# The radix-2 step of a second DFT stage moved onto the tokens, its constant factor stationary in eight 64x32 tiles of TensorE

## The chip, the cores and the metric

The kernel runs on one core of one Trainium2 chip. The metric is the device time of one execution in microseconds (us); lower is better. The median of three runs is compared, and one execution of each kernel is also recorded by the hardware profiler.

## The reference

```python
# x [8, 2496, 256], filt_r and filt_i [1249, 256]: all float32
X = np.fft.rfft(x, axis=1)
Y = X * (filt_r + 1j * filt_i)[None]
y = np.fft.irfft(Y, n=2496, axis=1)
x = y.reshape(8 * 2496, 256)
# soft mixture of experts: 8 experts, 4 slots each, 32 slots; phi [256, 32]
logits = x @ phi
d = softmax of logits over the 19968 tokens, one per slot
slot_out = relu((d.T @ x) @ w1) @ w2      # per expert: w1 [256, 1024], w2 [1024, 256]
c = softmax of logits over the 32 slots, one per token
out = c @ slot_out
```

## The kernel before

A DFT over 2496 = 39 x 64 tokens is computed as two stages. The first is a DFT over 39 for each of 64 residues; only 20 of its 39 frequencies t are needed, because x is real. The second is a DFT over 64 for each of the 20 t. The filter is applied to the spectra, and the logits and the slot inputs are taken from the spectra, so the inverse DFT is done only on the 32 slots' logits, not on the 256 channels.

The work of a batch entry b (8 of them, in order) is cut into these units:

- `split_x` (L299 to L307): ScalarE casts a tile of x to fp32r (`xh`, L305) and GpSimd takes the remainder `xl` (L306), 117 partitions by 512 elements each, 11 times for each b from 1 on.
- `s1_unit` (L309 to L324): the first DFT stage. Three fp32r matmuls of 512 columns (L316) accumulate `w1h*xh + w1l*xh + w1h*xl`; ScalarE copies the result to `at` (L317), and a DMA writes it to DRAM (`a_dram`, L321 to L324).
- `load_ash` (L331 to L338): a DMA reads two t back from `a_dram` with (residue, real or imaginary part) on the partitions.
- `x_unit` (L340 to L364): the second DFT stage for two t. The data tile `ash` is the stationary operand (128x128) and the constant 128x128 matrix `b` moves (128 columns), so the spectra stand in PSUM with channels on the partitions. VectorE multiplies them by the filter's real part (L360) and imaginary part (L361), VectorE or GpSimd (b from 6 on) adds (L363), and GpSimd subtracts (L364).
- `t_unit` (L366 to L390): four TensorE transposes turn the two t (L372), ScalarE copies them to `y` (L374), with frequencies on the partitions; at every second unit eight matmuls in 32-column tiles form logit spectra from phi (L383), and ScalarE copies them (L390).
- `chain(g)` (L396 to L607): for groups of b (0 and 1, 2 and 3, 4 and 5, 6, 7), the inverse DFT of the logits, the maximum, the exponentials, the forward DFT of the dispatch weights (`u2` L529, `dd` L537), and the slot sums (L575). It is a generator, advanced a few steps ("hops") per slot.

For b = 0 the first stage is done without DRAM by `first_unit` (L273 to L280) and `turn_ash` (L282 to L293).

One loop (L703 to L730) runs 80 slots, ten per b: slot n issues `load_ash` for slot n+5 (`ASH`), `split_x` for the next slot, `x_unit` of slot n, `s1_unit` for a later b (`AHEAD` 5 slots before), `t_unit` of slot n-2 (`LT`), and two or three hops. Instructions go to each engine's queue in an order that the framework plans from its own estimates; program order is not kept strictly. All DMAs are issued by SP's one queue. PSUM has eight banks, two for each of four pools (`ps_s1`, `ps_x`, `ps_t`, `ps_c`); a result of `x_unit` takes one bank, so two can be in flight.

After the loop come the last chains, the loads of w1 and w2 into freed buffers (L731 to L743), the experts (L762 to L800) and the output stage: softmax weights are turned and multiplied by the slot outputs (L859), copied (L868) and written (L891).

```python
# x_unit, before
pe.matmul(ps[:, 2 * k + dh].rearrange("q r c -> q (r c)"),
          ash[:, k, dh * P : (dh + 1) * P], C("b"), start=True, stop=True)
```

Of the kernel before, what the change touches and what calls it, by code (L numbers as in the profile page):

```python
# [9 lines left out]
F32 = mybir.dt.float32  # L10
# [33 lines left out]
KP = N2 + 2  # L44

XC = 4
XB = 3
AB = 5
AHEAD = 5
ASH = 5  # L50
LT = 2
HOPS = 2
LATE_HOPS = 3
# [3 lines left out]
X0S = 4  # L57
PA = 6
YB = 34
# [18 lines left out]
def bin_of(t, c):  # L78

    m = (c - t * pow(N1, -1, N2)) % N2  # L80
    return t + N1 * m


def shape_constants():
# [10 lines left out]
    th = 2 * np.pi * (np.outer(s2, N1 * np.arange(N2)) % N2) / N2  # L95
    co, si = np.cos(th), np.sin(th)
    bm = np.zeros((N2, 2, 2, N2))
    bm[:, 0, 0], bm[:, 0, 1], bm[:, 1, 0], bm[:, 1, 1] = co, -si, si, co
    bm = np.where(np.abs(bm) < 1e-12, 0.0, bm).reshape(P, P)
    wh = np.ones((P, 1))  # L100
    wh[0] = wh[N2 // 2] = 0.5
    minv = np.zeros((P, KP * 2))
    minv[:, 0:P] = SCALE * bm.T
    minv[:, P:] = np.tile(minv[:, P - 2 : P], (1, KP - N2))

# [15 lines left out]
    put("b", bm)  # L121
    put("wh", wh)
    put("minv", minv)
    put("minv0", wh * minv)
# [33 lines left out]
def filter_layout(filt):  # L158

    f = np.array([[bin_of(t, c) for c in range(N2)] for t in range(NT)])  # L160
    a = filt[np.where(f > SEQ // 2, SEQ - f, f)]
    a[0, N2 // 2 + 1 :] = 0
    return np.ascontiguousarray(a.reshape(NT, N2, 2, P).transpose(3, 0, 2, 1)).reshape(P, NT * 2 * N2)


def flip_runs(t):

    out = []
    for c in range(N2):
        if bin_of(t, c) > SEQ // 2:  # L170
            if out and out[-1][1] == c:
                out[-1] = (out[-1][0], c + 1)
            else:
                out.append((c, c + 1))
    return out


def x_layout(x):

    s1 = np.arange(N1)  # L180
    full = np.zeros((BATCH, P, NI, DIM), x.dtype)
# [22 lines left out]
def fft_soft_moe(ctx, tc, x, fr, fi, phi, w1, w2, cst, w1q, out):  # L204
# [12 lines left out]
    w1h = const.tile([KR, QP], F32R, name="w1h")  # L217
    w1l = const.tile([KR, QP], F32R, name="w1l")
    nc.vector.tensor_copy(w1h, w1q_t)
    nc.vector.tensor_tensor(out=w1l, in0=w1q_t, in1=w1h.bitcast(F32), op=ALU.subtract)  # L220

# [28 lines left out]
    fr_t = tabs.tile([P, NT, 2, 64], F32, name="fr_t")  # L250
    fi_t = tabs.tile([P, NT, 2, 64], F32, name="fi_t")
# [3 lines left out]
    def load_x(b, c):  # L255
        if b == 0:
            t = ypool.tile([P, 2, DIM], F32, tag="y", name=f"xt0_{c}")
            sp.dma_start(t, x[0, :, 2 * c : 2 * c + 2, :])
        else:
            t = proda.tile([P, XC, DIM], F32, tag="xt", name=f"xt{b}_{c}", bufs=XB)  # L260
            i0 = c * XC
            n = min(XC, NI - i0)
            sp.dma_start(t[:, 0:n, :], x[b, :, i0 : i0 + n, :])
        xts[b, c] = t

    def first_unit(u):

        xt = xts.pop((0, u))
        pool, tag = ((ps_s1, "s1"), (ps_x, "x"))[u % 2]
        ps = pool.tile([P, 2, 2, QP], F32, tag=tag, name=f"s0_{u}")  # L270
        for i in range(2):
            for dh in range(2):
                pe.matmul(ps[:, dh, i, :], xt[0:KR, i, dh * P : (dh + 1) * P], w1q_t, start=True, stop=True)  # L273
        n = min(2 * PK, N2 - 2 * PK * u)
        to = spec[:, :, :, 4 * PK * u : 4 * PK * u + 2 * n].rearrange("d h t k -> d h k t")
        src = ps.rearrange("d h i (j r t) -> d h (i j r) t", r=2, t=NT)[:, :, 0 : 2 * n]
        if u % 2 == 1:
            dve.tensor_copy(to, src)
        else:
            act.copy(to, src)  # L280

    def turn_ash(c):  # L282

        pt = ps_c.tile([P, 2, DIM], F32, tag="c", name=f"ash0_{c}")
        for k in range(2):
            for dh in range(2):
                pe.transpose(pt[:, k, dh * P : (dh + 1) * P], spec[:, dh, 2 * c + k, :], ident)
        ash = prod.tile([P, 2, DIM], F32, tag="ash", name=f"ash0_{c}", bufs=ASH)
        if c % 2 == 0:
            dve.tensor_copy(ash, pt)  # L290
        else:
            act.copy(ash, pt)
        ashs[0, c] = ash  # L293
# [3 lines left out]
    xhl = {}  # L297

    def split_x(b, u):  # L299

        c, k = divmod(2 * u, XC)
        xs = xts[b, c][0:KR, k : k + 2, :]
        xh = proda.tile([KR, 2, DIM], F32R, tag="xh", name=f"xh{b}_{u}", bufs=3)
        xl = proda.tile([KR, 2, DIM], F32R, tag="xl", name=f"xl{b}_{u}", bufs=3)
        act.copy(xh, xs)  # L305
        pool_e.tensor_tensor(out=xl, in0=xs, in1=xh.bitcast(F32), op=ALU.subtract)  # L306
        xhl[b, u] = xh, xl  # L307

    def s1_unit(b, u):  # L309
        if u == 0:  # L310
            a_dram[b] = scr.tile([N2, QR, DIM], F32, tag="a_dram", name=f"a_dram{b}")
        xh, xl = xhl.pop((b, u))
        ps = ps_s1.tile([QP, 2, DIM], F32, tag="s1", name=f"s1_{b}_{u}")
        at = proda.tile([QP, 2, DIM], F32, tag="at", name=f"at{b}_{u}", bufs=AB)
        for n, (w, xx) in enumerate(((w1h, xh), (w1l, xh), (w1h, xl))):
            pe.matmul(ps, w, xx, start=(n == 0), stop=(n == 2))  # L316
        act.copy(at, ps)  # L317
        k0 = PK * 2 * u
        dma = sp.dma_start
        if u < NH - 1:  # L320
            dma(a_dram[b][k0 : k0 + 2 * PK].rearrange("(i j) q d -> (j q) i d", j=PK), at)  # L321
        else:
            dma(a_dram[b][k0 : k0 + PK].rearrange("j q d -> (j q) d"), at[:, 0, :])
            dma(a_dram[b][k0 + PK], at[0:QR, 1, :])  # L324
# [6 lines left out]
    def load_ash(b, c):  # L331
        if b == 0:
            turn_ash(c)
            return
        t0 = 2 * c
        ash = prod.tile([P, 2, DIM], F32, tag="ash", name=f"ash{b}_{c}", bufs=ASH)
        sp.dma_start(ash, a_dram[b].rearrange("k (r t) d -> (k r) t d", t=NT)[:, t0 : t0 + 2, :])
        ashs[b, c] = ash  # L338

    def x_unit(b, c):  # L340

        t0 = 2 * c
        ash = ashs.pop((b, c))
        ps = ps_x.tile([P, 4, 2, 64], F32, tag="x", name=f"x_{b}_{c}")
        for k in range(2):
            for dh in range(2):
                pe.matmul(  # L347
                    ps[:, 2 * k + dh].rearrange("q r c -> q (r c)"),
                    ash[:, k, dh * P : (dh + 1) * P],
                    C("b"),  # L350
                    start=True,
                    stop=True,
                )
# [3 lines left out]
        if c % 2 == 0:  # L357
            yts[b, c // 2] = prod.tile([P, 2, 4, 2, 64], F32, tag="yt", name=f"yt_{b}_{c}")
# [565 lines left out]
```

## Time and profile before

| | before |
|---|---|
| runs (us) | 395.42, 400.12, 400.64; median 400.12 |
| profiled execution (us) | 398.73 |
| span in its profile (us) | 397.0 |
| mean granted TensorE clock | 0.95 |
| TensorE busy | 367.3 us, 93% of the span |
| VectorE, ScalarE, GpSimd busy | 67%, 54%, 52% of the span |
| moved by DMA | 103.67 MB, 261 GB/s over the span |

The span runs from the first to the last instruction; the execution's own time is 1.7 us longer. In the profile PE is TensorE's matmuls, PEld its weight loads (which overlap matmuls), DVE VectorE, ACT ScalarE, POOL GpSimd, SP the engine that issues DMAs. L347 is line 347 of the kernel. A float32 matmul stands in the profile as two records, each with a weight load of its own; a transpose or an fp32r matmul stands as one. A group's row gives busy time and the mean duration of one record; records of one group overlap, so that busy time is less than count times duration.

### The profile page before, as it was taken

Reading aid. Unit: us, or ns where it says so; the run is one execution under the profiler, and the core shown is the slowest. Engines: PE = TensorE matmul, PEld = TensorE weight load, DVE = VectorE, ACT = ScalarE, POOL = GpSimd, SP = SyncE. Lnnn points to the kernel's source line nnn. Section 1 sums busy time; section 2 is a strip of 40 time slices with the busy share of each in tenths; the row PEclk is TensorE's granted clock in tenths of the full one; section 3 lists DMA queues with packets and bytes.
Section 4 is the critical chain, followed back from the end, with each engine's and each line's share of the span. In section 5 each row is a group of like instructions: output and inputs, shape, how many; then the busy total and the mean of one; then the engine's idle time right before and its main releaser. Section 6 shows DMA issues by size and latency. Waiting matters only on the chain. (4 is left out here: it accounts for less than half of the span.)

```text
span 397.0 us, 11950 instructions
## 1 busy us (share of the span) xinstructions
PE 367.3 (93%) x4797; PEld 292.8 (74%) x4797; DVE 267.8 (67%) x465; ACT 215.3 (54%) x454; POOL 206.7 (52%) x258
## 2 busy tenths in 40 slices
PE   7998989998998999999989999999998899989980
PEld 6886778887686868887868688886766435889870
DVE  2496589874999928698996458994577222874570
ACT  2665858784667566757675343462455020654460
POOL 0499989994676666846945155662520000622200
PEclk9999999999999999999999999999999699985595
DMA  7997799997688886977886534423399993599796
GB/s 249 363 288 252 245 328 384 373 372 264 173 230 316 269 252 188 338 205 247 280 271 200 178 108 123 120 81 107 108 364 352 322 304 125 236 414 409 322 407 282
DMA packets 57481, 103.67 MB, mean 261 GB/s; under 512 B 5375, under 2 KB 34175, under 8 KB 55251
## 3 DMA queue, kind: packets, MB, share of 16 engines
q1 hardware_dynamic: 57427, 102.92, 77.1%
q8 instruction: 38, 0.62, 0.6%
q14 instruction: 16, 0.13, 0.1%
HBM read 62.78 MB, written 40.12 MB: 259 GB/s over the span
## 5 line engine op out<-in xcount | busy, mean ns | idle before, releaser
L306 POOL TENSOR_TENSOR xl<-xt,xh 117x512 fp32r<-117x512 f32 x77 | 102.0, 1332 | 17.8 <-ACT xh L305 17.3
L347 PE MATMUL x<-cst_t,ash 128*128 128x128 f32 x640 | 89.9, 281 | 3.2 <-issue 1.7
L347 PEld LDWEIGHTS x<-cst_t,ash 128*128 128x128 f32 x640 | 80.2, 191 | 12.8 <-issue 6.6
L364 POOL TENSOR_TENSOR yt<-yt,t 128x256 f32<-128x256 f32 x80 | 64.8, 812 | 39.4 <-DVE t L361 21.2
L360 DVE TENSOR_TENSOR yt<-x,fr_t 128x512 f32<-128x512 f32 x80 | 54.7, 683 | 29.7 <-PE x L347 16.4
L305 ACT CAST xh<-xt 117x512 fp32r<-117x512 f32 x77 | 47.6, 623 | 30.5 <-PE s L316 13.5
L374 ACT COPY y<-t 128x512 f32<-128x512 f32 x80 | 46.0, 590 | 29.1 <-PE t L372 27.4
L361 DVE TENSOR_TENSOR t<-x,fi_t 128x512 f32<-128x512 f32 x80 | 54.4, 680 | 2.4 <-POOL yt L364 2.2
L363 DVE TENSOR_TENSOR yt<-yt,t 128x256 f32<-128x256 f32 x60 | 51.0, 860 | 0.5
L372 PE MATMUL t<-cst_t,yt 128*128 128x128 f32 x320 | 48.5, 276 | 0.0
L317 ACT COPY at<-s 120x512 f32<-120x512 f32 x77 | 45.2, 587 | 4.6 <-PE s L316 4.1
L372 PEld LDWEIGHTS t<-cst_t,yt 128*128 128x128 f32 x320 | 37.3, 141 | 7.3 <-issue 2.7
L859 PE MATMUL out<-so_h,st 32*128 32x256 f32 x312 | 36.2, 355 | 3.1 <-ACT st L813 2.7
L316 PE MATMUL s<-xh,w1h 117*120 117x512 f32 x77 | 35.6, 462 | 2.1 <-ACT at L317 1.4
L859 PE MATMUL out<-so_l,st 32*128 32x256 f32 x312 | 34.3, 331 | 0.0
L825 POOL TENSOR_TENSOR c<-cl,r_all 117x352 f32<-117x352 f32 x8 | 6.2, 798 | 53.5 <-PE ct L839 46.8
L859 PEld LDWEIGHTS out<-so_h,st 32*128 32x128 f32 x312 | 29.8, 234 | 5.5 <-ACT st L813 3.1
L868 DVE COPY ob<-out 128x512 f32<-128x512 f32 (+1 forms) x40 | 25.4, 673 | 11.5 <-PE out L859 11.0
L316 PE MATMUL s<-xl,w1h 117*120 117x512 f32 x77 | 31.3, 407 | 0.0
L868 ACT COPY ob<-out 128x512 f32<-128x512 f32 (+1 forms) x40 | 21.5, 579 | 16.9 <-PE out L859 14.6
L316 PE MATMUL s<-xh,w1l 117*120 117x512 f32 x77 | 30.6, 397 | 0.0
L363 POOL TENSOR_TENSOR yt<-yt,t 128x256 f32<-128x256 f32 x20 | 16.2, 810 | 27.3 <-DVE t L361 15.0
(110 smaller groups left out, 566.3 us busy)
## 6 DMA issues: line engine op xcount, KB each, us to landing
xt<-in_x SPq DMA_DIRECT2D x35, 512.0 KB
ash<-a_dram SPq DMA_DIRECT2D x70, 256.0 KB
out<-ob SPq DMA_DIRECT2D x17, 1024.0 KB
a_dram<-at SPq DMA_DIRECT2D x70, 240.0 KB
w<-in_w SPq DMA_DIRECT2D x64, 256.0 KB
xt<-in_x SPq DMA_DIRECT2D x18, 256.0 KB
out<-ob SPq DMA_DIRECT2D x5, 512.0 KB
c_dram<-lg SPq DMA_DIRECT2D x2, 643.5 KB
```

The lines of the kernel that those rows point to most:

```text
L305: act.copy(xh, xs)
L306: pool_e.tensor_tensor(out=xl, in0=xs, in1=xh.bitcast(F32), op=ALU.subtract)
L316: pe.matmul(ps, w, xx, start=(n == 0), stop=(n == 2))
L347: pe.matmul(ps[:, 2 * k + dh].rearrange("q r c -> q (r c)"), ash[:, k, dh * P : (dh + 1) * P], C("b"), start=True, stop=True,)
L360: dve.tensor_tensor(out=yt, in0=ps, in1=frv, op=ALU.mult)
L361: dve.tensor_tensor(out=t2, in0=ps[:, :, ::-1, :], in1=fiv, op=ALU.mult)
L363: add.tensor_tensor(out=yt[:, :, 1, :], in0=yt[:, :, 1, :], in1=t2[:, :, 1, :], op=ALU.add)
L364: pool_e.tensor_tensor(out=yt[:, :, 0, :], in0=yt[:, :, 0, :], in1=t2[:, :, 0, :], op=ALU.subtract)
L372: pe.transpose(pt[:, k, dh, :], yt[:, c % 2, 2 * k + dh].rearrange("q r c -> q (r c)"), ident)
L374: act.copy(y, pt.rearrange("k p h d -> k p (h d)"))
L859: nc.tensor.matmul(prs[k][:, mm, :], st[q, n // 2, c0 : c0 + P], (so_h, so_l)[n % 2][q, :], start=(n == 0), stop=(n == 3),)
L868: copy(ob[:, nm * k : nm * (k + 1), :], prs[k])
```

## The change

The 64 residues k are taken as two halves, k and k + 32. The first butterfly of the DFT over 64 is done on the tokens, before the first stage: e = x(k) + x(k+32) and x(k) - x(k+32). The sums give the even frequencies of the second stage and the differences the odd ones, and each needs a sum over 32 residues x 2 parts = 64 rows only. In detail:

- `split_x` is replaced by `fold_x`: two tensor_tensor of 117 x 2 x 256 elements on GpSimd (for b = 0 the sum is on VectorE), the difference written in place. There is no cast to fp32r any more, and `s1_unit` uses one float32 matmul per result instead of three fp32r ones.
- `x_unit` handles four t: the constant `bx` is now the stationary operand in tiles of 64 rows x 32 columns (two halves of the rows x four column groups), the data `ash` moves with 256 columns. The spectra come out with frequencies on the partitions. The result takes two banks, and `ps_x` has one buffer of two banks instead of two of one.
- `y` is written by the filter's multiplications directly; `t_unit` turns it to channels on the partitions for the logits, with the same number of transposes and copies. Logits are taken for groups of two and three units, so with fewer, longer bursts and copies.
- The filter tables have the new layout; the signs of `fi_t` are set by ten ScalarE multiplications instead of GpSimd ones on column runs.
- In `chain`, `dd` is formed by 32-column tiles of `bd` stationary, and the half weight of two bins is applied to `lsb` by VectorE rather than by a second constant.
- There are 40 slots of twice the size; `AHEAD`, `ASH`, `LT`, hops and buffer counts are set anew.

```diff
-AHEAD = 5
-ASH = 5
-LT = 2
-HOPS = 2
-LATE_HOPS = 3
+EB = 2
+AHEAD = 3
+ASH = 2
+YT = 4
+LT = 1
+HOPS = 4
+LATE_HOPS = 6
...
-    ps_x = ctx.enter_context(tc.tile_pool(name="ps_x", bufs=2, space=PSUM))
+    ps_x_cm = tc.tile_pool(name="ps_x", bufs=1, space=PSUM)
+    ps_x = ps_x_cm.__enter__()
...
-        act.copy(xh, xs)
-        pool_e.tensor_tensor(out=xl, in0=xs, in1=xh.bitcast(F32), op=ALU.subtract)
+        e = proda.tile([P, 2, DIM], F32, tag="e", name=f"e{b}_{c}", bufs=EB)
+        eng = dve if b == 0 else pool_e
+        eng.tensor_tensor(out=e[0:KR, 0:n], in0=xt[0:KR, 0:n, 0], in1=xt[0:KR, 0:n, 1], op=ALU.add)
+        pool_e.tensor_tensor(out=xt[0:KR, 0:n, 1], in0=xt[0:KR, 0:n, 0], in1=xt[0:KR, 0:n, 1], op=ALU.subtract)
...
-        for n, (w, xx) in enumerate(((w1h, xh), (w1l, xh), (w1h, xl))):
-            pe.matmul(ps, w, xx, start=(n == 0), stop=(n == 2))
-        act.copy(at, ps)
+        for h, xe in enumerate(folds.pop((b, c))):
+            pe.matmul(ps[:, 0:n], w1q_t, xe[0:KR, 0:n], start=True, stop=True)
+            act.copy(at[:, 0:n], ps[:, 0:n])
...
-        ps = ps_x.tile([P, 4, 2, 64], F32, tag="x", name=f"x_{b}_{c}")
-        for k in range(2):
-            for dh in range(2):
-                pe.matmul(
-                    ps[:, 2 * k + dh].rearrange("q r c -> q (r c)"),
-                    ash[:, k, dh * P : (dh + 1) * P],
-                    C("b"),
+        ps = ps_x.tile([P, 2, 2, DIM], F32, tag="x", name=f"x_{b}_{c}")
+        for r in range(2):
+            for j in range(4):
+                for h in range(2):
+                    rows = slice(N2 * h, N2 * h + N2)
+                    pe.matmul(
+                        ps[NP * j : NP * j + NP, h, r],
+                        C("bx", NP * r, NP * r + NP)[rows],
+                        ash[rows, j],
...
-        dve.tensor_tensor(out=yt, in0=ps, in1=frv, op=ALU.mult)
+        dve.tensor_tensor(out=y, in0=ps, in1=frv, op=ALU.mult)
         dve.tensor_tensor(out=t2, in0=ps[:, :, ::-1, :], in1=fiv, op=ALU.mult)
...
+        for dh in range(2):
+            pt = ps_t.tile([P, 4, P], F32, tag="t", name=f"t_{b}_{c}_{dh}")
+            for k in range(4):
+                pe.transpose(pt[:, k, :], y[:, k // 2, k % 2, dh * P : (dh + 1) * P], ident)
+            act.copy(yt[:, dh], pt)
...
+            first = lsb[:, b2, 0]
+            dve.tensor_scalar(out=first, in0=first, scalar1=C("wh"), scalar2=None, op0=ALU.mult)
...
+        for c0 in range(0, 4, step):
+            pd = psum([P, step, NG4, nb * SLOTS], f"dd_{g}_{c0}")
+            for k in range(step):
+                for j in range(4):
+                    pe.matmul(
+                        pd[32 * j : 32 * j + 32, k],
+                        C("bd", 32 * (c0 + k), 32 * (c0 + k) + 32),
+                        u2[:, j::4],
...
-                pool_e.tensor_scalar(out=sl, in0=sl, scalar1=-1.0, scalar2=None, op0=ALU.mult)
+            act.mul(fi_t[:, c, h], fi_t[:, c, h], C("sg", 2 * c + h, 2 * c + h + 1))
```

More of the change, by code (lines that the diff above doesn't have):

```diff
@@ L56 @@
 WM = 1
-X0S = 4
+X0S = 1
 PA = 6
-YB = 34
+YB = 17
 WL = 5
@@ L93, in shape_constants, with turn @@
             w1[:, 1, t] = -np.sin(th)
[L95 to L99, printed above, removed]
+    def turn(k, f2):
+        th = 2 * np.pi * (np.outer(k, f2) % N2) / N2
+        co, si = np.cos(th), np.sin(th)
+        m = np.stack([np.stack([co, -si], 1), np.stack([si, co], 1)], 1)
+        return np.where(np.abs(m) < 1e-12, 0.0, m)
+    odd = 2 * np.arange(NP)
+    bx = np.stack([turn(np.arange(NP), odd + e) for e in range(2)]).reshape(P, 2 * NP)
+    bd = np.stack([turn(s2, odd + e) for e in range(2)], 2).reshape(P, P)
     wh = np.ones((P, 1))
-    wh[0] = wh[N2 // 2] = 0.5
+    wh[0] = wh[NP // 2] = 0.5
     minv = np.zeros((P, KP * 2))
-    minv[:, 0:P] = SCALE * bm.T
+    minv[:, 0:P] = SCALE * bd.T
     minv[:, P:] = np.tile(minv[:, P - 2 : P], (1, KP - N2))
+    sg = np.ones((4, NP, NG4, 2))
+    for t in range(NT):
+        for f2 in range(N2):
+            if t and bin_of(t, f2) > SEQ // 2:
+                sg[t % 4, f2 // 2, t // 4, f2 % 2] = -1.0
     blocks = []
@@ new lines, in first_unit @@
+    def first_unit(c):
+        n = min(2, NH - 2 * c)
+        nk = min(n * PK, NP - 2 * PK * c)
+        for h, xe in enumerate(folds.pop((0, c))):
+            pool, tag = ((ps_s1, "s1"), (ps_t, "t"))[h]
+            ps = pool.tile([P, 2, 2, QP], F32, tag=tag, name=f"s0_{c}_{h}")
+            for i in range(n):
+                for dh in range(2):
+                    pe.matmul(ps[:, dh, i, :], xe[0:KR, i, dh * P : (dh + 1) * P], w1q_t, start=True, stop=True)
+            k0 = N2 * h + 4 * PK * c
+            to = spec[:, :, :, k0 : k0 + 2 * nk].rearrange("d h t k -> d h k t")
+            src = ps.rearrange("d h i (j r t) -> d h (i j r) t", r=2, t=NT)[:, :, 0 : 2 * nk]
+            if h == 1:
+                dve.tensor_copy(to, src)
+            else:
+                act.copy(to, src)
@@ new lines, in turn_ash @@
+    def turn_ash(c):
+        ash = prod.tile([P, 4, DIM], F32, tag="ash", name=f"ash0_{c}", bufs=ASH)
+        for m in range(2):
+            pt = ps_c.tile([P, 2, DIM], F32, tag="c", name=f"ash0_{c}_{m}")
+            for k in range(2):
+                for dh in range(2):
+                    pe.transpose(pt[:, k, dh * P : (dh + 1) * P], spec[:, dh, 4 * c + 2 * m + k, :], ident)
+            if m == 0:
+                dve.tensor_copy(ash[:, 0:2], pt)
+            else:
+                act.copy(ash[:, 2:4], pt)
@@ L373, in t_unit @@
[L373 to L390 removed]
+        y = ys[b, c]
@@ L654, in fft_soft_moe @@
         load_tables(next(tabs_next))
-    for u in range(NH):
+    for u in range(IPS):
+        fold_x(0, u)
         first_unit(u)
```

287 lines of the change are left out of this document (119 added, 168 removed).

## The prediction, made before the changed kernel was run

> **What bounds the kernel now.** I read the table of stretches first, because the page's 93% is a mean over stages with different limits. Its columns are the length, busy time (and records) of PE, PEld, DVE, ACT and POOL, the granted clock, the DMA share and GB/s.
>
> ```profile
> 0.00:20.00 20.00, 17.46 (x112) 15.22 (x113) 7.06 (x11) 9.76 (x13) 5.25 (x15) 1.00 0.90 306
> 20.00:40.00 20.00, 18.43 (x143) 15.20 (x145) 14.81 (x22) 11.53 (x22) 20.00 (x34) 1.00 0.86 270
> 40.00:220.00 180.00, 173.37 (x2138) 140.35 (x2141) 143.12 (x220) 122.22 (x253) 130.61 (x121) 1.00 0.84 274
> 220.00:272.00 52.00, 51.11 (x853) 43.18 (x842) 41.87 (x73) 21.88 (x48) 28.18 (x38) 1.00 0.42 120
> 290.00:318.00 28.00, 23.46 (x378) 15.91 (x381) 17.04 (x57) 10.92 (x34) 0.00 (x0) 0.88 1.05 348
> 318.00:338.00 20.00, 19.54 (x224) 8.96 (x224) 4.47 (x9) 3.47 (x8) 1.33 (x2) 1.00 0.67 207
> 20.00:272.00 252.00, 242.90 (x3121) 198.73 (x3120) 199.80 (x315) 155.63 (x323) 178.79 (x192) 1.00 0.76 242
> ```
>
> The slot loop, from about 20 to 272 us (the first and last records of L347 below show it), is TensorE's: PE is busy 242.9 of 252 us, VectorE 199.8, GpSimd 178.8, ScalarE 155.6, and the clock is full. Only in 20 to 40 us is another engine full: POOL, 20.00 of 20, and there PE loses 8%. DMA stands at 0.84 in the long middle part. After the loop come the last chains with the expert weights' loads (DMA 1.05), the experts and the output; the change touches little there, and I take it that these 125 us (272 to 397) keep their length and move forward with the loop's end. So the question is what the change does to TensorE's work in the loop, and which other limit stands next.
>
> The groups give the prices, and the timeline shows how bursts follow one another; its columns are start and duration in us, and a start less the one before it is what a burst takes from the engine.
>
> ```profile
> L347 PE MATMUL x<-cst_t,ash 128*128 128x128 f32 x640 | 89.9, 281 | 3.2 <-issue 1.7
> L347 PEld LDWEIGHTS x<-cst_t,ash 128*128 128x128 f32 x640 | 80.2, 191 | 12.8 <-issue 6.6
> L306 POOL TENSOR_TENSOR xl<-xt,xh 117x512 fp32r<-117x512 f32 x77 | 102.0, 1332 | 17.8 <-ACT xh L305 17.3
> L364 POOL TENSOR_TENSOR yt<-yt,t 128x256 f32<-128x256 f32 x80 | 64.8, 812 | 39.4 <-DVE t L361 21.2
> L360 DVE TENSOR_TENSOR yt<-x,fr_t 128x512 f32<-128x512 f32 x80 | 54.7, 683 | 29.7 <-PE x L347 16.4
> L361 DVE TENSOR_TENSOR t<-x,fi_t 128x512 f32<-128x512 f32 x80 | 54.4, 680 | 2.4 <-POOL yt L364 2.2
> L363 DVE TENSOR_TENSOR yt<-yt,t 128x256 f32<-128x256 f32 x60 | 51.0, 860 | 0.5
> ...
> 19.55 1.06 PE L347 MATMUL x<-cst_t,ash 128*128 128x128 f32 x8
> ...
> 151.92 0.39 PE L316 MATMUL s<-xh,w1h 117*120 117x512 f32 x1
> 152.15 0.39 PE L316 MATMUL s<-xh,w1l 117*120 117x512 f32 x1
> 152.38 0.39 PE L316 MATMUL s<-xl,w1h 117*120 117x512 f32 x1
> 152.61 0.27 PE L416 MATMUL ltr<-cst_t,lt 128*128 128x128 f32 x1
> ...
> 153.25 0.65 PE L383 MATMUL l<-yt,phi_t 128*32 128x128 f32 x16
> 153.83 2.05 PE L347 MATMUL x<-cst_t,ash 128*128 128x128 f32 x16
> 155.64 0.47 PE L316 MATMUL s<-xh,w1h 117*120 117x512 f32 x1
> ...
> 269.70 2.41 PE L347 MATMUL x<-cst_t,ash 128*128 128x128 f32 x16
> 275.08 4.52 PE L575 MATMUL s<-y,dd 128*32 128x256 f32 x80
> 279.54 0.66 PE L416 MATMUL ltr<-cst_t,lt 128*128 128x128 f32 x4
> ...
> 324.53 1.92 PE L770 MATMUL h<-w,sit 128*32 128x512 f32 x16
> 326.38 0.66 PE L780 MATMUL ht<-cst_t,hsb 128*128 128x128 f32 x4
> ```
>
> **Prices on TensorE.** A burst in 32-column tiles has four tiles at work at once: the 80 records of L575 (256 columns) take 279.54 - 275.08 = 4.46 us, and the 16 of L770 (512 columns) 1.85 us. The 16 short ones of L383 (128 columns) take 0.58 us. Taking 0.13 us as the start of a burst makes the three agree: (4.46 - 0.13) x 4 / 80 = 0.217 us for a record of 256 columns by itself, (1.85 - 0.13) x 4 / 16 = 0.43 us for 512, (0.58 - 0.13) x 4 / 16 = 0.11 us for 128. So a float32 record costs 0.85 ns a column, and tiles that work side by side divide it.
>
> **x_unit, the term that gains.** Now 16 records (four t) take 155.64 - 153.83 = 1.81 us, which over 640 records is 72.4 us; the weight loads of the group are busy for 80.2 us. I take the middle, 76 us, or 1.9 us for four t. Afterwards four t are 16 matmuls, 32 records of 256 columns, on eight tiles. If all eight work at once, a burst is 32 x 0.217 / 8 + 0.13 = 1.0 us, 40 us in all. If the two row halves take turns, so that only four columns of tiles work at once, it is 32 x 0.217 / 4 + 0.13 = 1.86 us, 75 us. No row of this trace shows row halves side by side with column tiles. I take 1.0, because the four column tiles of L575 already divide the time by four and the two halves read different partitions and write different banks: **-36 us** (bounds -41 and +2).
>
> The Trainium skill ("TensorE: Matmul & The Clock Gate", Part 3, Measured speedup vs the span model) gives 6.32 times for nine tiles and 10.6 for sixteen, not the full factor. By an estimate from it, 5.6 for eight, the burst would be 32 x 0.217 / 5.6 = 1.24 us, some 8 to 10 us less gain, and the time about 394. L575 with its almost full four speaks against so large a loss; eight tiles this trace cannot show.
>
> **s1_unit, the term that loses.** Three fp32r matmuls take 152.61 - 151.92 = 0.69 us; 77 of them 53 us. One float32 matmul of 512 columns is two records, 0.86 us by the price above; there are 70 of 512 and 14 of 256 columns, as much as 77 full ones: 66 us. **+13 us** (bounds 11 and 18, the upper if each record starts anew with 0.06 of the 0.13 us).
>
> **Logits and the rest of TensorE.** The 640 records of L383 stay, in 16 bursts instead of 40: 24 x 0.13 = **-3 us**. Transposes stay at 320. `dd` has the same columns x tiles, divided by four tiles: nothing, at most 1 us either way.
>
> **The head.** For b = 0 TensorE now waits for a transfer of 512 KB instead of 256 KB (0.25 MB more at 306 GB/s: 0.8 us) and for a fold, on GpSimd 1.33 us by the row of L306; the sixth difference is the last thing its tile waits for. **+2 us** (0 to 5; GpSimd's six differences, 8 us, lie beside TensorE's stage-one matmuls).
>
> **What moves to other engines.** ScalarE loses its 77 casts. GpSimd's folds have the elements of `xl` (77 x 512), so 102 us stay; its y work falls from 100 operations of 256 to 50 of 512 elements, 81 to 50 x 1.33 = 67 us, and its sign flips go. VectorE's multiplications go from 160 of 512 to 80 of 1024 elements:
>
> ```profile
> L868 DVE COPY ob<-out 128x512 f32<-128x512 f32 x38 | 24.8, 687 | 11.5 <-PE out L859 11.0
> L868 DVE COPY ob<-out 128x256 f32<-128x256 f32 x2 | 0.7, 414 | 0.0
> L546 DVE TENSOR_SCALAR dd<-dd,cst_t 128x32 f32<-128x32 f32 x2 | 0.5, 237 | 2.6 <-ACT dd L544 2.6
> ```
>
> From 256 to 512 elements a reading of PSUM grows by 0.27 us, so 1024 take 687 + 2 x 273 = 1.23 us: 80 x 1.23 = 98 instead of 109 us. The adds, 30 of 512, take 0.8 to 1.7 us each, 1.4 by what 0.86 x 2 less one start would be: 42 instead of 51. So VectorE's 199.8 us in the loop become 180, GpSimd's 178.8 about 162. The new `lsb` multiplication costs 0.24 to 0.41 us on a chain, in the loop beside other work and once in the tail. DMA carries the same bytes; its 0.84 x 180 us become 0.93 of a stretch shorter by some 18 us, which fits, barely. The early weights have 45 places instead of 40, worth nothing as long as the chain, not the weights, releases L770.
>
> **Sum.** -36 + 13 - 3 + 2 = -24 us. I do not take it whole: with TensorE at 220 instead of 243 us, VectorE (180), GpSimd and DMA (0.93) stand closer, and the buffers are tighter. The result of x_unit has one buffer of two banks, so the next burst waits for both multiplications; behind it in TensorE's queue stand `s1_unit`, the transposes and the hops. The tile `xt` is free only when its matmuls are done, and only two `e` exist, so a fold can wait for TensorE, with the y subtraction queued behind it on GpSimd and the transposes behind that. The nearest row for the price is 20 to 40 us, where PE loses 8% beside a full POOL; in the middle part it loses 4%. I take 4% more of the loop, 10 us (bounds 0 and 24). So -14: the profiled execution goes from 398.7 to 384.5, and the median of the runs, 1.4 us above it, from 400.1 to about **386 us**.
>
> **Rivals.** *The gain is eaten by VectorE.* With one buffer x_unit and VectorE can take turns: 1.0 us of burst, 180 / 40 = 4.5 us of VectorE, and the time in which VectorE waits for TensorE; L360's row has 29.7 us of idle time, 0.74 us per new slot. That is 6.24 us a slot, against 252 / 40 = 6.3 now: 250 + 2 for the head, about 400. For it: VectorE is already at 79%, and its chain work depends on TensorE. Against it: a slot has over 4 us of TensorE work that does not need this buffer. The Trainium skill ("TensorEngine Tiling (Array Packing)", PSUM Bottleneck) has the rule that tiling speeds up TensorE and not the evacuation of PSUM; by L360 and L361 the evacuation here even gets 10% cheaper.
>
> *The row halves do not work side by side* (the change then does not do what it says): -1 + 13 - 3 + 2 = +11 with nothing to hide it, since TensorE is the bound: about 411. It decides from a burst of 1.9 - (13 - 3 + 2) / 40 = 1.6 us on; below that TensorE's work shrinks. For it: nothing in the trace shows eight tiles. Against it: the division by four is nearly complete for column tiles.
>
> *All of the sum arrives, and slots get no new waits*: 398.7 - 24 + 1.4 = 376.
>
> **How the numbers follow.** Forecast with partial give-back (376 to 392): 0.5; the whole sum or more (366 to 376): 0.14; the gain eaten (392 to 404): 0.22; the halves in turn (404 to 416): 0.14. 2% of 400 us, 8 us, is about what a measurement here can tell from no change. Faster by more than that holds the first two, 0.64; within 2% the third and part of the last, 0.23; slower 0.13. The range for 8 in 10 leaves out the slow end and a little of the fast one: 370 to 407.
>
> **What would show it.** Right: the x bursts of 32 records start to next start in 1.0 to 1.25 us; `s1` records of 512 columns follow at 0.43 us; PE in the loop near 220 us; the loop ends near 258 instead of 272 us and the tail is as long as before. VectorE eaten: x bursts short, but x waits for VectorE's second multiplication and PE under 90% in the loop. Halves in turn: bursts of 1.8 us. I would be wrong in another way if the tail changed its length, if DMA reached 1.0 and ash tiles came late, or if the head grew by more than 5 us.

## The result, and the profile after

| | before | after |
|---|---|---|
| median (us) | 399.75 (4 runs) | 428.76 (4 runs, 424.54 to 432.75) |
| ratio to before, 95% interval | | 1.0717 [1.0611, 1.0823] |
| span in the profile (us) | 397.0 | 422.8 |
| last transpose of the loop starts (us) | 285.7 | 310.7 |
| mean granted clock | 0.95 | 0.96 |

The change costs 29 us, 7%, where 14 us less were forecast. The profiled executions took 398.73 and 424.54 us, so the profiles show 25 to 26 of the 29. The run at 432.75 us stands at a lower clock (0.925) and is not in the ratio. The page of the changed kernel, its shares of busy time and its chain by lines:

```profile
span 422.8 us, 12898 instructions
PE 358.2 (85%) x5508; PEld 225.7 (53%) x5508; DVE 259.0 (61%) x368; ACT 181.7 (43%) x373; POOL 198.2 (47%) x192
...
DMA xt<-in_x 10%; PE s L317 9%; PE x L348 6%; PE t L373 6%; PE out L864 5%; PE s L580 4%; DVE d L498 3%; PE v L433 3%; PE s L286 3%; PE l L385 3%; DMA out<-ob 3%; PE u L516 2%; POOL y L363 2%; PE dd L544 2%; POOL e L273 2%
```

Every engine is busy for a smaller share than before (PE 93%, VectorE 67%, GpSimd 52%), and none is full: the kernel now waits. At the head of the chain stands a load, `xt<-in_x`, with 10%. The stretches of both kernels, before first, with the columns of the prediction's first table:

```profile
20.00:286.00 266.00, 256.75 (x3358) 208.04 (x3357) 204.51 (x326) 161.77 (x336) 183.05 (x198) 1.00 0.73 233
```

```profile
20.00:40.00 20.00, 19.58 (x161) 9.61 (x159) 9.15 (x10) 10.71 (x22) 14.86 (x13) 1.00 0.89 271
40.00:100.00 60.00, 52.90 (x602) 27.39 (x598) 35.55 (x35) 28.76 (x54) 49.53 (x41) 1.00 0.94 302
20.00:311.00 291.00, 256.95 (x4002) 148.67 (x4001) 192.40 (x228) 128.82 (x256) 168.49 (x133) 0.98 0.67 210
```

The stretch from 20 us to the last transpose is 25 us longer, and so is the span; the clock is nearly full (0.98). PE's busy time is the same in both, 257 us, which at first sight says that TensorE's work did not shrink. It did: records that are in flight while the next one waits count as busy. The work is read from starts (here and below "work" is the sum of bursts, each by its spacing to the next as priced in the prediction, and "waits" is the rest of the stretch up to the last transpose; both are estimates from all records of the trace, and they move by several us with how a burst is priced). Before: 256 us of work and 11 of waits. After: 240 and 50. By this estimate **the work fell by 16 us and the waits grew by 40**; what is measured is their sum, the 25 us.

The ends of the stretch and the first expert matmul, in the timeline of before and then of after:

```profile
285.74 0.60 PE L372 MATMUL t<-cst_t,yt 128*128 128x128 f32 x4
...
317.93 1.49 PE L770 MATMUL h<-w,sit 128*32 128x512 f32 x12 [0.32 <-DVE sit L760]
```

```profile
168.02 1.02 PE L317 MATMUL s<-xt,w1q_t 117*120 117x512 f32 x2
168.88 1.02 PE L317 MATMUL s<-e,w1q_t 117*120 117x512 f32 x2
169.83 1.09 PE L348 MATMUL x<-ash,cst_t 64*32 64x256 f32 x32
170.85 0.69 PE L317 MATMUL s<-xt,w1q_t 117*120 117x512 f32 x1
...
310.66 1.09 PE L373 MATMUL t<-cst_t,y 128*128 128x128 f32 x8 [0.59 <-POOL y L363]
...
345.30 1.92 PE L775 MATMUL h<-w,sit 128*32 128x512 f32 x16 [0.32 <-DVE sit L765]
```

From the last transpose to the end of the span it is 111.3 us before and 112.1 after: the tail kept its length by this mark. By the prediction's own mark, the last x burst, the loop ends at 305.2 instead of 271.8 us, where some 258 were forecast, and what follows is 117.6 us instead of 125.2. And a burst of 32 records in eight tiles takes 170.85 - 169.83 = 1.02 us and a matmul of 512 columns of the first stage 168.88 - 168.02 = 0.86, as forecast. So the loss lies in waits of the loop. The table of waits of after (engine, instruction, what it waited for: us in total, times, the longest):

```profile
DVE y L359 <- PE x L348: 43.4, 23, 6.3
...
POOL e L273 <- DMA xt<-in_x: 22.2, 16, 3.1
PEld t L373 <- POOL y L363: 21.2, 19, 2.3
POOL e L273 <- PE s L317: 19.5, 5, 7.9
```

VectorE waits for TensorE, 43.4 us. Of the opposite, x bursts of TensorE that wait for VectorE, the view has 0.4 us (it puts some of these waits down elsewhere; see C below). GpSimd's sums wait for loads of `xt` and for `e` tiles that TensorE still reads; TensorE's transposes wait for GpSimd's subtraction. The chain of waits shows from 55 us on how these hang together (start, duration, what):

```profile
55.96 5.49 DMA xt<-in_x
...
61.58 1.29 POOL e L273
62.87 0.07 issue
62.94 1.28 POOL xt L274
64.21 1.24 POOL y L363
65.45 0.04 issue
65.50 1.09 PE t L373 x8
66.59 0.86 PE s L317 x2
67.45 0.33 PE ltr L418 x3
67.78 0.86 PE s L317 x2
```

The issues of these loads, of which these are the first and the last of fourteen, and the two that belong to the tile above, stand in SP's timeline:

```profile
39.56 0.36 SPq L262 DMA_DIRECT2D xt<-in_x  x1
...
55.96 0.37 SPq L262 DMA_DIRECT2D xt<-in_x  x1
...
68.70 0.35 SPq L262 DMA_DIRECT2D xt<-in_x  x1
...
91.08 0.35 SPq L262 DMA_DIRECT2D xt<-in_x  x1
```

This is a ring. A tile `xt` is loaded (5.5 us) and summed and differenced in place (2.6); then GpSimd's queue goes on with a `y` subtraction (1.2), TensorE with the transposes that waited for it (1.1), and only then with the first stage that reads the tile. At 68.70 the tile is free and is loaded again, 12.7 us after the load before. There are three tiles (`XB`), so a tile comes every third of a turn: 51.5 us for 13 intervals, 4.0 us each, a turn of 11.9. The ring sets the pace in this early part. From about 100 us on the loads come every 5.6 us (19 intervals from 98.2 to 205.0), and there the ring is not what paces them, as the run with six tiles shows below.

### The profile page after: what moved, and what is told of

It reads as the page before. It is cut to its first block, busy times and chain, and to the rows that moved or that the text cites. A ratio compares the mean times of both kernels' runs of the same rounds, so it can differ in the third digit from the quotient of the medians.

```text
span 422.8 us, 12898 instructions
## 1 busy us (share of the span) xinstructions
PE 358.2 (85%) x5508; PEld 225.7 (53%) x5508; DVE 259.0 (61%) x368; ACT 181.7 (43%) x373; POOL 198.2 (47%) x192
## 4 chain that ended last, share of the span: by engine, by line
PE 55%; DVE 14%; DMA 13%; POOL 7%; ACT 4%; issue 3%; SPq 0%; DVEq 0%; POOLq 0%; ACTq 0%
DMA xt<-in_x 10%; PE s L317 9%; PE x L348 6%; PE t L373 6%; PE out L864 5%; PE s L580 4%; DVE d L498 3%; PE v L433 3%; PE s L286 3%; PE l L385 3%; DMA out<-ob 3%; PE u L516 2%; POOL y L363 2%; PE dd L544 2%; POOL e L273 2%
## 5 line engine op out<-in xcount | busy, mean ns | idle before, releaser
L359 DVE TENSOR_TENSOR y<-x,fr_t 128x1024 f32<-128x1024 f32 x40 | 48.9, 1221 | 47.7 <-PE x L348 43.4
L273 POOL TENSOR_TENSOR e<-xt 117x512 f32<-117x512 f32 (+1 forms) x42 | 52.0, 1237 | 53.7 <-DMA xt<-in_x 22.2
L374 ACT COPY yt<-t 128x512 f32<-128x512 f32 x80 | 44.0, 590 | 68.4 <-PE t L373 68.1
L363 POOL TENSOR_TENSOR y<-y,t 128x512 f32<-128x512 f32 x40 | 55.9, 1397 | 27.2 <-DVE t L360 27.2
L274 POOL TENSOR_TENSOR xt<-xt 117x512 f32<-117x512 f32 (+1 forms) x48 | 59.7, 1245 | 11.0 <-DVE e L273 8.8
L319 ACT COPY at<-s 120x512 f32<-120x512 f32 (+1 forms) x84 | 46.0, 552 | 42.1 <-PE s L317 39.2
L348 PE MATMUL x<-ash,cst_t 64*32 64x256 f32 x1280 | 56.2, 383 | 5.9 <-issue 2.7
L373 PE MATMUL t<-cst_t,y 128*128 128x128 f32 x320 | 46.9, 287 | 11.7 <-POOL y L363 11.3
L373 PEld LDWEIGHTS t<-cst_t,y 128*128 128x128 f32 x320 | 36.0, 145 | 29.4 <-POOL y L363 21.2
L360 DVE TENSOR_TENSOR t<-x,fi_t 128x1024 f32<-128x1024 f32 x40 | 48.6, 1214 | 0.0
L317 PE MATMUL s<-xt,w1q_t 117*120 117x512 f32 (+1 forms) x84 | 42.1, 583 | 0.2
L362 POOL TENSOR_TENSOR y<-y,t 128x512 f32<-128x512 f32 x10 | 13.1, 1310 | 39.9 <-DVE t L360 38.5
L516 PE MATMUL u<-cst_t,d 117*32 117x60 f32 (+1 forms) x704 | 16.4, 226 | 10.9 <-ACT u L526 8.1
```

Of the source, the lines that this page charges most:

```text
L273: eng.tensor_tensor(out=e[0:KR, 0:n], in0=xt[0:KR, 0:n, 0], in1=xt[0:KR, 0:n, 1], op=ALU.add)
L274: pool_e.tensor_tensor(out=xt[0:KR, 0:n, 1], in0=xt[0:KR, 0:n, 0], in1=xt[0:KR, 0:n, 1], op=ALU.subtract)
L317: pe.matmul(ps[:, 0:n], w1q_t, xe[0:KR, 0:n], start=True, stop=True)
L319: act.copy(at[:, 0:n], ps[:, 0:n])
L348: pe.matmul(ps[NP * j : NP * j + NP, h, r], C("bx", NP * r, NP * r + NP)[rows], ash[rows, j], start=True, stop=True,)
L359: dve.tensor_tensor(out=y, in0=ps, in1=frv, op=ALU.mult)
```

## The experiments

The theories, with the letters that the expectations use. **A**: the ring of `xt` tiles. **B**: the transposes come one slot after their spectra (`LT` = 1, two before), too soon after GpSimd's subtraction, which stands behind the folds. **C**, the main rival: `ps_x` has one buffer, so that TensorE and VectorE take turns. **D**: the slots are coarser, with four or six hops in a row. **E**, formed later: there are too few `y` tiles. Times are medians with the ratio to the kernel before, run on the same chip (its medians were 397 to 398). Gains against the changed kernel are differences of such medians where nothing else is said; its own interval is 4 us to either side.

**More x tiles, and more distance.** Three more `xt` tiles; the number of early table loads stays as it was. Beside it `LT` alone, and then both.

```diff
-XB = 3
+XB = 6
     for k in range(XB):
         next_x()
-        load_tables(next(tabs_next))
+        if k < 3:
+            load_tables(next(tabs_next))
-LT = 1
+LT = 2
```

> Edit: XB = 6 instead of 3 on the changed kernel (six buffers for the x tiles instead of three; all else as it is). Theory A (ring of the x tiles: a tile is free only when its first-stage matmuls are done, its load then takes over 5 us, and the folds, the y subtraction queued behind them on GpSimd, the transposes and the next first-stage matmuls wait in a ring): folds no longer wait for x loads (22 us of GpSimd's idle time now), the loop (284 us from the first to the last x burst) falls by 10 to 20 us, time 409 to 419 us. Theory B (the wait for the y subtraction is a matter of distance, with one slot between the spectra and their transposes): under 4 us less, 425 to 429. Theory C (one buffer of two banks for the spectra): no change, 427 to 430.

> Edit: LT = 2 instead of 1 on the changed kernel (the transposes of a unit come two slots after its spectra instead of one). Theory B: TensorE's transposes no longer wait for the y subtraction (about 20 us of gaps before transposes now), time 405 to 418. Theory A: the folds still wait for x loads and for TensorE, so only the part of the wait that was not paid elsewhere goes: 421 to 428. Theory C: no change or slower, 427 to 432.

> Edit: XB = 6 and LT = 2 together on the changed kernel. If the ring of the x tiles (A) and the distance of the transposes (B) are two causes, their gains (16 and 9 us) add: 402 to 406. If both shorten the same ring, the second adds little: 408 to 412. Under both, what is left above 398 is neither.

`XB` = 6: 412.31, 1.0332 [1.0252, 1.0412]. `LT` = 2: 419.9, 1.0533 [1.0463, 1.0603]. Both: 405.84, 1.0195 [1.0128, 1.0261]. So 16 us of the loss are the ring's, 9 the distance's when alone and 6 on top of the ring (15, 7 and 5 by the ratios). The first lies in the range of A, the third in that of two causes; `LT` = 2 alone fell between the ranges of B and A. A and B both hold, A weighs more. The waits and the stretches of the kernel with both:

```profile
DVE y L359 <- PE x L348: 30.3, 23, 3.2
...
POOL e L273 <- PE s L317: 27.1, 11, 9.3
...
PEld t L373 <- POOL y L363: 7.0, 10, 1.2
```

```profile
22.00:100.00 78.00, 76.55 (x995) 42.59 (x994) 53.49 (x54) 41.17 (x80) 72.77 (x57) 1.00 0.96 335
220.00:286.00 66.00, 57.29 (x1208) 38.48 (x1191) 46.80 (x63) 24.51 (x51) 25.63 (x20) 0.95 0.30 90
```

In this kernel the loads are issued from 40.07 to 84.00 us in the same 13 intervals, 3.4 us each instead of 4.0, by SP's timeline:

```profile
40.07 0.38 SPq L262 DMA_DIRECT2D xt<-in_x  x1
...
84.00 0.35 SPq L262 DMA_DIRECT2D xt<-in_x  x1
```

The wait for loads has gone from the head of the list, the transposes' wait fell from 21.2 to 7.0 us, and up to 100 us PE is busy for 98% instead of some 90%. In its place the folds wait longer for `e` (27.1), and the end of the loop, from 220 us on, has 9 us without any matmul, where before had 1 in 52. From 100 us on the loads come every 5.6 us here too (15 intervals from 99.7 to 183.7), so the ring is a matter of the first 100 us: with both edits the first x burst of b = 3 starts at 109.6 instead of 122.5 us, and these 13 us are most of the 19 by which the last one comes earlier.

The Trainium skill ("Perfetto Trace Analysis", Optimization Strategy) has the rule that one gap which repeats on the engine that should be full can mean too few buffers for the next tile; the 16 us for three tiles agree.

**Is it GpSimd's queue?** The butterfly is left out for b from 1 on (both halves of the tile go to the first stage as they are), with three tiles and `LT` = 1, and then with six and 2.

```diff
+        if b > 0:
+            folds[b, c] = xt[:, :, 0], xt[:, :, 1]
+            return
```

> Edit: for b from 1 on the butterfly is left out: the first-stage matmuls read the two halves of the x tile as they came, so GpSimd has no folds (three x buffers, as in the changed kernel). If the waits come through GpSimd's queue, where the y subtraction stands behind folds that wait for x loads (A with GpSimd as the link): the loop loses the waits before transposes, time 400 to 410. If the ring is the load alone (three buffers, a load of over 5 us after the matmuls that free one): TensorE waits for the load directly, time 415 to 425. Theory C: no change, 426 to 430.

> Edit on the changed kernel: XB = 6, LT = 2, and the butterfly left out for b from 1 on (the matmuls read the halves as they came). With buffers and distance mended, what GpSimd's 100 us of folds still cost: if the first 100 us, where GpSimd is 95% busy and DMA at 0.95, are GpSimd's, 395 to 402; if they are the DMA's or what remains lies after 220 us, 403 to 407.

408.81, 1.0272 [1.0155, 1.039]; and 400.18, 1.008 [1.0048, 1.0112]. Without the folds, but with three tiles, 18 us come back: the steps between load and release, or the queue that they make on GpSimd, are what makes the ring long; the run removes both. With six tiles the folds cost only 5 us more than nothing. The stretches of the second:

```profile
22.00:100.00 78.00, 77.40 (x1036) 43.59 (x1034) 49.68 (x55) 41.94 (x81) 23.86 (x14) 1.00 0.97 341
220.00:282.00 62.00, 51.79 (x1139) 34.68 (x1136) 40.11 (x56) 22.66 (x47) 24.21 (x19) 0.97 0.26 79
```

Up to 100 us TensorE is full by its busy time, 77.4 of 78. The end of the loop is not: 10 of 62 us are empty. So even without any fold the kernel does not get under the one before, and what is left lies late. The time lies in the range for a GpSimd that holds the first 100 us, but not for that reason: there PE gains under 1 us over the kernel with folds (76.55 to 77.40), and most of the 5 us come between the first x bursts of b = 3 (106.9 instead of 109.6 us) and b = 4 (150.9 instead of 158.5).

**Is it the one PSUM buffer (C)?** A second buffer for `ps_x` needs two banks; they were taken from `ps_t` and `ps_c`, and a control has only these two cut. Beside that, the second multiplication reads `y` instead of PSUM, which changes what is multiplied, not how much; the buffer is then free after the first.

```diff
-    ps_t = ctx.enter_context(tc.tile_pool(name="ps_t", bufs=2, space=PSUM))
-    ps_c = ctx.enter_context(tc.tile_pool(name="ps_c", bufs=2, space=PSUM))
+    ps_t = ctx.enter_context(tc.tile_pool(name="ps_t", bufs=1, space=PSUM))
+    ps_c = ctx.enter_context(tc.tile_pool(name="ps_c", bufs=1, space=PSUM))
...
-    ps_x_cm = tc.tile_pool(name="ps_x", bufs=1, space=PSUM)
+    ps_x_cm = tc.tile_pool(name="ps_x", bufs=2, space=PSUM)
...
-        dve.tensor_tensor(out=t2, in0=ps[:, :, ::-1, :], in1=fiv, op=ALU.mult)
+        dve.tensor_tensor(out=t2, in0=y[:, :, ::-1, :], in1=fiv, op=ALU.mult)
```

> Edit: ps_t and ps_c with one buffer each instead of two, ps_x with one buffer as in the changed kernel; the control for the next run. All theories: slower than the changed kernel, as each transpose tile and each chain tile waits for its copy: 432 to 450.

> Edit: ps_t and ps_c with one buffer each, ps_x with two buffers of two banks. To be read against the control with one buffer of ps_x. Theory C (an x burst must wait for both multiplications of the one before): 12 us or more faster than the control. Theories A and B: within 5 us of the control.

> Edit: the second multiplication reads y from SBUF instead of the spectra in PSUM (the imaginary part's product is then formed from the wrong operand); the PSUM buffer of x_unit is held for one multiplication (1.2 us) instead of two (2.4 us). Theory C: the gaps before x bursts (15 us) shrink, 415 to 424. Theories A and B: no change within 4 us, 425 to 432, as VectorE's work stays the same.

The control took 514.11, 1.2879 [1.2749, 1.301], with the second buffer 521.07, 1.3067 [1.2961, 1.3174]. The control was expected at 432 to 450, and the pair settles nothing, because something else governs both: TensorE's transposes now wait for ScalarE's copies (10.9 us in the control's trace, a wait that the changed kernel's list does not have), and 48 of the control's 89 us of longer span lie behind the first expert matmul. The other kernel says more: 428.18, 1.0761 [1.0693, 1.0828], no gain, though the buffer is held for one multiplication instead of two. Its group and wait show what else changed:

```profile
L360 DVE TENSOR_TENSOR t<-y,fi_t 128x1024 f32<-128x1024 f32 x40 | 58.8, 1469 | 2.5
```

```profile
PEld t L373 <- POOL y L363: 32.0, 22, 4.3
```

The multiplication itself took 1.47 us in the mean instead of 1.21, 10 us over 40, and VectorE's additions 1.20 instead of 0.99, 6 us over 30. A gain of some us could hide behind that; the 29 us of the loss could not.

The changed kernel's own trace settles C better. A burst that waits for the buffer starts right when the second multiplication (L360) of the unit before ends. Two such pairs of it, one in the middle and one late:

```profile
163.05 1.22 DVE L360 TENSOR_TENSOR t<-x,fi_t 128x1024 f32<-128x1024 f32 x1
165.85 1.09 PE L348 MATMUL x<-ash,cst_t 64*32 64x256 f32 x32
...
241.72 1.21 DVE L360 TENSOR_TENSOR t<-x,fi_t 128x1024 f32<-128x1024 f32 x1
243.04 1.10 PE L348 MATMUL x<-ash,cst_t 64*32 64x256 f32 x32 [1.58 <-issue]
```

The first burst comes 1.58 us after the buffer is free, the second 0.1 us. Of the 28 bursts that follow another one up to 235 us only two come within 0.3 us of it, and the first fourteen leave at least 1.2 us. Of the eleven after 235 us seven start 0.10 us behind the multiplication, and TensorE is idle for 5.5 us before them in sum. C is not the main cause. Late in the loop it takes a part, some 5 us by this reading, that no run here took away by itself.

**The subtraction of y on VectorE**, which takes it out of the queue behind the folds:

```diff
-        pool_e.tensor_tensor(out=y[:, :, 0, :], in0=y[:, :, 0, :], in1=t2[:, :, 0, :], op=ALU.subtract)
+        dve.tensor_tensor(out=y[:, :, 0, :], in0=y[:, :, 0, :], in1=t2[:, :, 0, :], op=ALU.subtract)
```

> Edit: the y subtraction on VectorE instead of GpSimd for all b (three x buffers, LT = 1). If the transposes wait because the subtraction stands in GpSimd's queue behind folds: those waits go, VectorE has 30 to 40 us more, time 410 to 420. If VectorE with the one spectra buffer is what sets the loop (C): slower than the changed kernel, 432 to 450.

420.11, 1.0541 [1.0463, 1.0618]: 9 us (7 by the ratios), as much as `LT` = 2. That it is by the same link (B) fits. It speaks against C too, since VectorE got more work and the kernel became no slower. The ring stays, as its waits say:

```profile
POOL e L273 <- DMA xt<-in_x: 52.7, 20, 7.8
```

**The first stage by itself.** The kernel before, with one plain float32 matmul for three fp32r ones, and without casts:

```diff
-        for n, (w, xx) in enumerate(((w1h, xh), (w1l, xh), (w1h, xl))):
-            pe.matmul(ps, w, xx, start=(n == 0), stop=(n == 2))
+        pe.matmul(ps, w1q_t, xs, start=True, stop=True)
```

> Edit, on the kernel before: one part of the change alone, the first stage as one float32 matmul instead of three fp32r ones, so neither the cast to fp32r on ScalarE nor the remainder on GpSimd. By the prediction's term TensorE gets 13 us more in a loop that it bounds, and GpSimd loses 102 us of work there: if the loop before is TensorE's alone, 408 to 413; if GpSimd took part in the bound (it was full from 20 to 40 us and 70% busy in the loop), less: 398 to 407.

410.4, 1.0359 [1.0307, 1.0411], 13 us over its neighbour before at 397.15:

```profile
20.00:284.00 264.00, 255.72 (x3046) 187.97 (x3045) 177.33 (x315) 122.06 (x250) 81.74 (x114) 0.99 0.74 230
```

GpSimd's work is more than halved (81.7 us) and ScalarE's cut by a quarter, and the time follows TensorE alone, 255.7 of 264. The +13 of the sum is right, and the loop of the kernel before is TensorE's.

**Third `e` tile, finer hops.** Five `xt` tiles, three `e` tiles, `LT` = 2; and, on the kernel with six tiles and `LT` = 2, half of each slot's hops right behind `x_unit`, the rest in the old place (theory D).

```diff
-EB = 2
+EB = 3
...
             x_unit(*divmod(n, CPB))
+            hop_slot(n, 0)
...
-        hop_slot(n)
+        hop_slot(n, 1)
```

> Edit on the changed kernel: XB = 5, EB = 3, LT = 2. Against XB = 6, EB = 2, LT = 2 (405.8 us), where folds waited 27 us for TensorE to give an e tile back: if that wait holds the y subtraction up as the loads did, 398 to 403; if it was paid by nothing behind it, 405 to 408.

> Edit on the changed kernel: XB = 6, LT = 2, and the hops of a slot in two halves, one right behind x_unit and one at the slot's end, as in the kernel before, where half as many hops followed each unit of half the size. Theory D (coarser slots: four or six chain steps in a row, each waiting for another engine, leave TensorE without other work; from 222 to 286 us PE lost 9 of 64): 396 to 402. If the order within a slot matters little because the planner reorders it: 404 to 408.

402.12, 1.014 [1.0103, 1.0178]: the folds' wait for `e` falls from 27.1 to 14.5 us, worth some 2 us by the ratios against the kernel with six `xt` tiles and two `e`, which the intervals do not tell from nothing; this is the best of the changed family that computes all. 403.65, 1.0186 [1.0147, 1.0225]: finer hops do nothing that could be told from noise, so D is not what is left.

**Copies from VectorE to ScalarE.** Three copies of `chain` (`lsb`, `v`, `u2`) go to ScalarE, in the best kernel, in the kernel before, without folds, and with `PA` = 8 instead of 6, which leaves the addition to `y` on VectorE for the last two b instead of giving it to GpSimd.

```diff
-            dve.tensor_copy(v[:, s0 : s0 + n, :], pv[:, 0:n])
+            act.copy(v[:, s0 : s0 + n, :], pv[:, 0:n])
```

> Edit on the changed kernel: XB = 5, EB = 3, LT = 2 (402.1 us without more), and the chains' three copies out of PSUM (lsb, v, u2; some 20 us) on ScalarE instead of VectorE. If stretches where the chains fill VectorE take what is left of the gain: 394 to 399. If what is left is latency between engines (each step of a chain waiting for the one before), the copies cost the same elsewhere: 400 to 404.

> The same three copies moved to ScalarE in the kernel before. VectorE is full there in 118 to 140 us, with PE at 20.4 of 22. If TensorE alone sets that loop: 395 to 399, no change. If VectorE's full stretches take part in the bound before: 388 to 394.

> Edit on the changed kernel: XB = 5, EB = 3, LT = 2, the copies on ScalarE and the butterfly left out for b from 1 on. Takes GpSimd's folds and VectorE's copies away together. If GpSimd in the first 100 us and VectorE later are the two limits behind TensorE: 387 to 393. If the loop is held by the last 70 us, which have no folds (PE at 16 to 17 of 20 there): 396 to 401.

> As the run with XB = 5, EB = 3, LT = 2 and the copies on ScalarE, and PA = 8: for the last two batch entries the addition stays on VectorE, beside GpSimd's subtraction, instead of ahead of it on GpSimd. If the way from spectra to transposes (two multiplications and two GpSimd operations one behind the other, 5 us) holds the last 70 us: 4 to 8 us less than that run. If not: the same within 2 us.

In the changed kernel 410.41, 1.0348 [1.0263, 1.0433], 8 us slower than without the move, which neither theory expected; in the kernel before 395.24, 0.9928 [0.988, 0.9976]; without folds 399.71, 1.009 [1.0046, 1.0135]; with `PA` = 8 406.88, 1.0243 [1.0164, 1.0322], some 4 us less than the first, which the intervals do not tell from nothing. The third lies in the range for a loop that is held by its last 70 us. The stretch of the first, beside that of the kernel without the move:

```profile
20.00:290.00 270.00, 246.27 (x3967) 145.97 (x3965) 166.61 (x189) 138.37 (x282) 165.89 (x129) 0.97 0.68 222
```

```profile
20.00:282.00 262.00, 244.39 (x3979) 144.22 (x3977) 181.54 (x221) 125.38 (x251) 165.60 (x129) 0.99 0.70 229
```

VectorE has 15 us less and the loop is 8 us longer. VectorE's load as a whole is not what is left of the loss. That ScalarE's copies of `at` and `yt`, on which the rings wait too, come later behind the moved copies is argued, not shown.

**More y tiles (E).** In the kernel with `LT` = 2 the x bursts stop three times for 16 to 20 us (the longest stops of the kernel before are 11.5 and 12.3 us). The last one in its timeline:

```profile
273.83 1.10 PE L348 MATMUL x<-ash,cst_t 64*32 64x256 f32 x32 [0.85 <-PE t L373]
...
288.95 4.52 PE L580 MATMUL s<-y,dd 128*32 128x256 f32 x80 [0.23 <-ACT dd L551]
289.65 1.23 DVE L359 TENSOR_TENSOR y<-x,fr_t 128x1024 f32<-128x1024 f32 x1 [0.65 <-PE s L580]
...
293.99 1.09 PE L348 MATMUL x<-ash,cst_t 64*32 64x256 f32 x32
```

VectorE takes the result of the burst at 273.83 only at 289.65, after the first slot sums (L580) have released a `y`. In the kernel before `y` was written by the copy after the transposes; now `x_unit`'s multiplication writes it, a step earlier, and holds the one PSUM buffer until it can. Three more `y` tiles, in a pool of their own:

```diff
-LT = 1
+LT = 2
+YX = 3
-        y = ypool.tile([P, 2, 2, DIM], F32, tag="y", name=f"y_{b}_{c}")
+        ypl, yt_ = (yxp, "yx") if (b * CPB + c) % (YB + YX) < YX else (ypool, "y")
+        y = ypl.tile([P, 2, 2, DIM], F32, tag=yt_, name=f"y_{b}_{c}")
```

> Edit on the changed kernel: LT = 2 and three more y buffers, 20 instead of 17 (in a pool of their own), three x buffers as in the changed kernel. To be read against LT = 2 alone (419.9 us). Theory E (y is now written by x_unit itself, so x_unit stops when the buffers are full: two b of a chain's group, the next b and two units of the one after, until that chain's slot sums give the first back; in the changed kernel the spectra of one unit wait in PSUM from 277 to 294 us and the next x burst comes only at 299): 404 to 412, with x bursts going on to the end of b = 3, 5 and 7. If those stretches are held by the chain's own steps and not by the buffers: 417 to 422.

> What the experiments point to, together, on the changed kernel: XB = 4, EB = 3, LT = 2, 20 y buffers, PA = 8, and to make room AB = 4 and YT = 3. If the x ring, the e tiles, the distance and the y buffers are separate waits: 388 to 395, faster than the kernel before. If the wait for y only covers the chains' own time: 400 to 405, as with XB = 5, EB = 3, LT = 2 without more y (402.1).

414.64, 1.0412 [1.0346, 1.0478], 5 us under `LT` = 2 alone: the stops of 16 to 20 us are gone (one of 9.4 is left), but the gain lies between the two expectations. The second kernel has all at once as far as the memory goes (`XB` 4, `EB` 3, `YX` 3, `PA` 8, paid with `AB` 4 and `YT` 3): 420.8, 1.053 [1.0468, 1.0592], a miss. Its loop ends early (last transpose at 296.3), but the first expert matmul comes only at 342.0, 45.6 us later instead of 34. Its loads of `w` wait for the slot sums:

```profile
SPq L694 <- PE s L583: 19.4, 2, 18.7
```

But it is not the weights that hold that matmul: in the trace it starts 0.05 us after VectorE's copy of `sit` ends (341.91), the last step of the chains. The slot sums of b = 4 and 5 come at 301.9 us, after the last transpose, where the kernel with `LT` = 2 has them at 288.95, 17 us ahead of its last transposes; so the loop ran ahead of the chains, and the chains set the end. Which of the changed settings slowed them is not told apart.

## Why the prediction was wrong, point by point

**The bursts: right.** 1.02 us against 1.0 forecast and the bounds 1.0 to 1.86; so the halves of the rows do not take turns. 32 x 0.217 / 1.02 is a factor of 6.8. The estimate from the Trainium skill ("TensorE: Matmul & The Clock Gate", Part 3, Measured speedup vs the span model), 5.6 and 1.24 us, was too cautious for these tiles.

**-36 for `x_unit`: too large.** By spacings the group took some 71 us before, not the 76 that I chose between spacing and weight loads' busy time, and some 43 after, with restarts: -28. Busy time of weight loads should not have entered.

**+13 for the first stage: right**, in the changed kernel by spacing (52.4 to 65.6) and by itself in the altered kernel before. **Logits -3, head +2: right** (22.4 to 19.1; first x burst at 21.2 instead of 19.5 us). Terms that I had at nothing add some 3 us. So TensorE's work fell by some 16, not 26. (The last line of the sum is off by 0.2: 398.7 less 14 is 384.7.)

**The step that failed is the give-back: "I take 4% more of the loop, 10 us (bounds 0 and 24)".** It was some 40 us. The upper bound was the whole gain, as if a change could at worst lose what it brings. That holds only while TensorE stays the bound. Here the change put a longer ring beside it (load, two folds behind each other, matmuls, and between them the `y` subtraction and the transposes), and a ring's pace does not depend on how much TensorE's work shrank. I named this very path in the text and priced it from the row 20 to 40 us of before, where PE lost 8%, a row in which that ring did not exist. What it needed was one turn of the ring, added up. The runs give it: 11.9 us for three tiles, one every 4.0, where the loop takes one every 3.4 once there are six. That is 0.6 us on each of 42 folds, 25 us, had it held all through the loop. It held for the first 100 us, and 16 were shown.

**The rivals.** VectorE and the one buffer: falls as the main cause by the bursts that start 1.2 us and more after the buffer is free, by the run with the short hold, by VectorE's 43.4 us of waiting for TensorE, and by the moved copies. Its sign "PE under 90% in the loop" came true all the same (257 of 291 us), so it could not tell the rivals apart; and behind 235 us the wait for the one buffer is there, some 5 us. The halves in turn: falls by the burst. The fourth way, a slower loop by new rings, was the one that happened, and was no rival of mine. **DMA and the tail**: DMA stood at 0.94 from 40 to 100 us, as full as forecast, and at 0.67 over the loop; the tail kept its length. "PE in the loop near 220 us" fell, and would have been a poor sign in any case, since busy time counts waiting records.

**What stays open.** Of the 40 us of added waits the rings of `xt`, `e` and `LT` account for 18 by spacing, an estimate (50 to 32 in the best kernel; in the time it is 23 us by the ratios). What is left lies mostly behind 220 us, also without folds: the `y` tiles explain a part (5 us shown, with three `xt` tiles), the one PSUM buffer may explain another (some 5 us, read from the trace, not tried), the rest is not told apart. No version of the change that computes all beats the kernel before; the only kernel below it is the kernel before with three copies moved, by 0.7%, less than 2%.

## What to carry to other kernels

Before counting time freed on the bounding engine as gain, go through every set of buffers that the change alters, add up one turn (load, each step until release, and what stands in between in the queues), divide by the number of buffers, and compare that with the pace that the forecast needs. A change that moves a step to the loaded tile, or writes a tile one step earlier, lengthens a turn even where every instruction got cheaper. The price of such a wait has no upper bound in the gain; a row from before, where the ring does not exist in this form, cannot give it. Whether one buffer holds its producer can be read off a trace: compare the producer's start with the end of the last reader before it.

## What the runs showed of the hardware that was not expected

Eight tiles of 64x32 work nearly at once: 32 float32 records of 256 columns in 1.02 us, where one by itself is priced at 0.217 by the prediction's rows. VectorE's multiplication of 128x1024 with both inputs in SBUF (the run with the short hold) took 1.22 us in the mean of the 16 that ran while GpSimd was idle and 1.73 in the mean of the 16 that ran for over nine tenths of their time beside GpSimd's work; with one input in PSUM, in the changed kernel, all 40 took 1.20 to 1.22 us. Cutting two PSUM pools from two buffers to one cost 85 us; from 400 us on the granted clock was 0.56 in that run. The same three copies, moved to ScalarE, took 8 us in one kernel and gave 3 in the other.
